# One decode block: cache and weight loads as long runs per partition, four heads per tile, one ring of buffers

## The chip, the cores and the metric

The kernel runs on one core of one Trainium2 chip. TensorE (PE) multiplies, VectorE (DVE) and ScalarE (ACT) do the elementwise work, GpSimd (POOL) builds a few constants, and SyncE (SP) issues the loads. All loads go from HBM to the on-chip memory (SBUF, 128 partitions) over 16 DMA engines. The metric is the device time of one execution in microseconds (us), as the median of several; lower is better.

## The reference

Two requests (B = 2) with one token each (D = 640) pass one transformer block whose norms are modulated by a condition `c`. Attention has 32 heads of 192 and looks at the last 1024 of 4096 cached positions.

```python
mod = (silu(c) @ w_mod).reshape(2, 6, 1, 640)      # sa, ca, ga, sb, cb, gb
h = layernorm(x) * (1 + ca) + sa
q = h @ wq                                          # 640 x 6144
k, v = k_cache[:, :, 3072:], v_cache[:, :, 3072:]   # 2 x 32 x 1024 x 192 each
p = softmax(einsum('bhqd,bhkd->bhqk', q, k) * 192 ** -0.5)
x = x + ga * (einsum('bhqk,bhkd->bhqd', p, v) @ wo) # wo 6144 x 640
h = layernorm(x) * (1 + cb) + sb
return x + gb * ((gelu(h @ w_gate) * (h @ w_up)) @ w_down)   # inner width 1536
```

All inputs are bf16. The part of the caches that is read is 50.3 MB; w_mod is 4.9 MB, wq and wo 7.9 MB each, and the three feed-forward weights 5.9 MB together.

## The kernel before

The kernel is written as lists of operations, one list per engine, in program order. A small tracker (`_Sched`, lines 27 to 101) adds the semaphore waits from what each operation reads and writes: buffers, ring slots and the eight banks of PSUM (the accumulation memory). Each engine runs its list strictly in order, SP too: a load that waits for a buffer holds every load behind it.

**Load order.** SP issues all loads through `k_dma` (line 242): c, x, the first third of w_mod (shift and scale of the first norm), wq in four column blocks, the rest of w_mod, then the caches through a ring, then wo in four row blocks, gate, up, and w_down in three pieces. wq and wo share one buffer (`r1`), w_mod and the feed-forward weights another (`r3`). A weight row with index k * 128 + p lies on partition p, so a partition gets one run of bytes per row and block.

**Ring.** `declare_ring` (line 260) fills 10 slots. One load brings one head of K or of V for both requests: partition p gets 8 consecutive positions (8 x 192 elements) of each request, two runs. K slots are released by the multiplies, V slots by the product with V.

**Start.** c and x are transposed on PE, the modulation is 150 matmuls with 128x128 weight tiles and 2 columns (line 328), then comes the norm. `q_unit` (line 347) computes q already repeated on all partitions: the normed x is copied into 128 columns (`hbc`, line 341), and five matmuls of 512 columns give 512 elements of q for one request (line 359); ACT copies them to `qbc`.

**A group** (16 of them) is two heads of both requests, four units. For each unit DVE multiplies K by q elementwise (line 396), and PE adds up over the 192 elements in three matmuls of 512 columns with an identity (line 408), which leave 64 sums per position; DVE adds these up for all four units at once (line 415). Then follow the maximum over the free axis (419), a transpose on PE (421), the maximum over the partitions (426), a diagonal matrix on ACT (428), its broadcast on PE (430), the subtraction (435) and the exponential (438). `p_pv` (line 441) multiplies with V, four units in four column strips of PE, and also sums the weights (454). One group later the result is divided (467, 469) and brought into rows by eight small matmuls (477, 478). `filler` (line 366) puts a unit of q, or later four matmuls whose result is not used, into gaps of PE. In the loop at line 488 the steps of three neighbouring groups are interleaved.

**End.** wo (line 546, 240 matmuls), the second norm, gate and up (line 564, 120), gelu, w_down (line 583, 60), a transpose of the result and its store.

Of the kernel before, what the change touches and what calls it, by code (L numbers as in the profile page):

```python
# [103 lines left out]
def bass_adaLN_cond__sliding_block_cached__geglu_ffn__decode_kernel(  # L104
# [13 lines left out]
    dbg=None,  # L118
):
    P = 128  # L120
# [5 lines left out]
    assert B == 2 and Dh == 192 and D % P == 0 and W % P == 0 and H % 2 == 0 and F % P == 0  # L126
    KT = D // P
    J = W // P
    NQ = H * Dh
    NT = NQ // P  # L130
    NG = H // 2
    FC = F // P
    SCALE = float(Dh) ** -0.5
    EPS = 1e-5
    GC = 512 // J
    NCH = Dh // GC
    assert J % 2 == 0 and GC * NCH == Dh and 2 * Dh + J <= 512
    ON = 2 * Dh

    NS = 10 if dbg is None else 8  # L140
    NP = 3
    HPC = 8 if H % 8 == 0 else 2
    NWQ = H // HPC
    CQ = HPC * Dh
    TPC = 12 if NT % 12 == 0 else 3
    NWO = NT // TPC
    WD_SPLIT = [FC // 2, FC - FC // 2 - max(1, FC // 6), max(1, FC // 6)] if FC >= 6 else [FC]
    WD_SPLIT = [n for n in WD_SPLIT if n > 0]
    QW = 512
    NQC = (NQ + QW - 1) // QW  # L150
    QUP = min(2 * NQC, 2 * ((3 * 2 * Dh + QW - 1) // QW))
    ND = 4

    es = ExitStack()
    with es:
        S = _Sched(nc, es)
        sb = lambda name, shape, dt: es.enter_context(nc.sbuf_tensor(name, shape, dt))

        r1 = sb("r1", [P, KT * NQ], BF16)
        wq_v = r1[:, :].rearrange("p (k n) -> p k n", k=KT)  # L160
        wo_v = r1[:, :].rearrange("p (t n) -> p t n", t=NT)
        R3N = max(KT * 6 * D + KT * 2 * P, 2 * KT * F + FC * D)
        r3 = sb("r3", [P, R3N], BF16)
        wm_v = r3[:, 0:KT * 6 * D].rearrange("p (k n) -> p k n", k=KT)
        hbc_v = r3[:, KT * 6 * D:KT * 6 * D + KT * 2 * P].rearrange("p (k b m) -> p k b m", k=KT, b=2)
# [3 lines left out]
        qbc = sb("qbc", [P, 2, NQ], BF16)  # L169
        ring = sb("ring", [P, NS, 2, J, Dh], BF16)  # L170
        prod = sb("prod", [P, NP, J, Dh], BF16)
# [4 lines left out]
        sel = sb("sel", [P, 8], BF16)  # L176
        xr = sb("xr", [2 * KT, P], BF16)
        cr = sb("cr", [2 * KT, P], BF16)
        scT = sb("scT", [P, KT, 2], BF16)
        X2 = sb("X2", [P, 2, KT, 2], F32)  # L180
# [3 lines left out]
        modT = sb("modT", [P, 6, KT, 2], F32)  # L184
        opc = sb("opc", [P, 2, KT, 2], F32)
        lnt = sb("lnt", [P, 2, KT, 2], F32)
        hT = sb("hT", [P, KT, 2], BF16)
        S_sb = sb("S_sb", [P, 2, 4, J], F32)
        Sb_sb = sb("Sb_sb", [P, 2, 4, J], F32)
        M1 = sb("M1", [P, 2, 4], F32)  # L190
        gmn = sb("gmn", [4, 2], F32)
        diag = sb("diag", [4, 2, 4], F32)
        E_sb = sb("E_sb", [P, 2, 4, J], BF16)
        den = sb("den", [P, 2], F32)
        junk = sb("junk", [P, 2, J], F32)
        rden = sb("rden", [P, 2], F32)
        On = sb("On", [P, 2, ON], BF16)
        oT = sb("oT", [P, NT, 2], BF16)
        h2T = sb("h2T", [P, KT, 2], BF16)
        gl = sb("gl", [P, FC, 2], F32)  # L200
        aT = sb("aT", [P, FC, 2], BF16)
        fin = sb("fin", [P, 2, KT, 2], F32)
        orow = sb("orow", [2 * KT, P], BF16)
        ps = es.enter_context(nc.psum_tensor("ps", [P, 8, 512], F32))

        BK_S = (0, 1, 2, 3)
        BK_T = 4
        FTC = 256
        BK_O = 5
        OTC = 2 * Dh + J + 8  # L210
        BK_Q = (6, 7)
# [7 lines left out]
        sem_wm = [S.sem("d_wm%d" % i) for i in range(2)]  # L219
        sem_wq = [S.sem("d_wq%d" % i) for i in range(NWQ)]  # L220
        sem_wo = [S.sem("d_wo%d" % i) for i in range(NWO)]
# [5 lines left out]
        dbg_sems = []  # L227
# [13 lines left out]
        def k_dma(dst, src):  # L241
            return lambda e: e.dma_start(dst, src)  # L242
# [7 lines left out]
        for i in range(NWQ):  # L250
# [4 lines left out]
                                    writes=["wm1"], name="ld_wm1"))  # L255

        ring_state = {"next": 0, "done": set()}
        NITEM = 4 * NG

        def declare_ring(consumed=()):  # L260
            ring_state["done"].update(consumed)
# [407 lines left out]
```

## Time and profile before

| | |
|---|---|
| median of 3 runs | 212.14 us (209.55 to 212.56) |
| profiled execution: span, first to last instruction | 207.9 us |
| profiled execution: its own time | the page gives none beside the span |
| read from HBM | 76.88 MB, 370 GB/s over the span |
| busy: PE, DVE, ACT | 134.0, 110.4, 43.5 us |
| mean granted clock of TensorE | 0.875 |

The profile is one execution recorded by the hardware. A group row gives line, engine, operation, output <- inputs, shape and count, then busy time and mean length of one, then idle time before it and what ended it. A row by stretches gives start:end, length, busy time and count for PE, PE weight loads, DVE, ACT and POOL, then the granted clock of TensorE, the DMA share, and GB/s. A row in order of time gives start, length, engine, line and operation, and how long the engine had been idle.

### The profile page before, as it was taken

The page shows a single profiled execution, that of the slowest core. Times are in us where ns is not written, and L with a number is a line of the kernel's source. Part 1 is how long each engine was busy: PE and PEld are TensorE (multiplying, and loading weights), DVE is VectorE, ACT ScalarE, POOL GpSimd, SP SyncE. Part 2 cuts the span into 40 slices and gives each one's busy share as a digit, 9 for nine tenths or more (in the row PEclk, how much of TensorE's full clock was granted, in tenths as well). Part 3 has the DMA queues.
Part 4 walks back from the last instruction along what each step waited for, and adds up shares of the span by engine and source line. Part 5 has one row for each costly group of instructions (what it writes and reads, how often), then busy time and mean ns, then how long its engine had stood idle before and what let it go on. Part 6 is the DMA issues. An engine that isn't in the chain of part 4 may idle for free.

```text
span 207.9 us, 3411 instructions
## 1 busy us (share of the span) xinstructions
PE 134.0 (64%) x1424; PEld 68.0 (33%) x1441; DVE 110.4 (53%) x176; ACT 43.5 (21%) x132; POOL 1.2 (1%) x9
## 2 busy tenths in 40 slices
PE   0229500696668869769687696696696694743443
PEld 0213200532333334324333243243243242643342
DVE  0050000439487876977869779779779765000300
ACT  2023300011423222232323221121121112400300
POOL 2000000000000000000000000000000000000000
PEclk9999955559999999999999999999999999555555
DMA  4999999999999999999999999999999999999990
GB/s 125 407 403 401 402 415 408 401 400 404 399 392 382 410 348 400 377 352 413 358 356 410 337 331 395 404 403 401 402 403 397 397 363 362 361 365 400 394 330 26
DMA packets 30523, 77.10 MB, mean 371 GB/s; under 512 B 1324, under 2 KB 9004, under 8 KB 30508
## 3 DMA queue, kind: packets, MB, share of 16 engines
q1 hardware_dynamic: 30508, 76.89, 97.7%
q8 instruction: 11, 0.18, 0.4%
q14 instruction: 4, 0.03, 0.0%
HBM read 76.88 MB, written 0.00 MB: 370 GB/s over the span
## 4 chain that ended last, share of the span: by engine, by line
PE 32%; SPq 32%; DVE 16%; DMA 13%; ACT 4%; issue 2%
SPq L242 32%; DVE S_sb L415 14%; PE ps L408 14%; DMA ring<-in_A_k_cache_dram 8%; DMA r<-in_B_w_down_dram 5%; PE ps L450 5%; PE ps L359 5%; PE ps L373 2%; ACT qbc L363 2%; PE ps L430 2%; PE ps L421 2%; PE ps L477 1%; DVE M L419 1%; ACT L438 1%; ACT E_sb L438 1%
## 5 line engine op out<-in xcount | busy, mean ns | idle before, releaser
L396 DVE TENSOR_TENSOR prod<-ring,qbc 128x1536 bf16<-128x1536 bf16 x64 | 59.3, 947 | 5.0 <-DMA ring<-in_A_k_cache_dram 5.0
L408 PE MATMUL ps<-prod,ident_b 128*128 128x512 bf16 x192 | 53.6, 391 | 1.8 <-DVE prod L396 1.8
L415 DVE TENSOR_REDUCE S_sb<-ps 128x32 f32<-128x2048 f32 x16 | 36.7, 2291 | 3.7 <-PE ps L408 3.7
L359 PE MATMUL ps<-r 128*128 128x512 bf16 x110 | 30.0, 413 | 4.3 <-DVE r L341 3.7
L363 ACT ACTIVATE qbc<-ps 128x512 bf16<-128x512 f32 x24 | 14.3, 597 | 43.8 <-PE ps L359 43.8
L408 PEld LDWEIGHTS ps<-prod,ident_b 128*128 128x128 bf16 x192 | 16.7, 99 | 18.4 <-issue 4.8
L421 PE MATMUL ps<-ident_f,M 128*4 128x128 f32 x16 | 4.3, 271 | 26.2 <-DVE M L419 26.2
L359 PEld LDWEIGHTS ps<-r 128*128 128x128 bf16 x120 | 11.9, 105 | 18.2 <-issue 4.6
L328 PE MATMUL ps<-scT,r 128*128 128x2 bf16 x150 | 4.3, 165 | 18.3 <-DMA r<-in_w_mod_dram 18.3
L450 PE MATMUL ps<-ring,E_sb 128*2 128x384 bf16 x256 | 13.7, 336 | 3.2 <-ACT E_sb L438 3.2
L381 DVE TENSOR_SCALAR opc<-modT 128x10 f32<-128x10 f32 x1 | 0.2, 173 | 24.7 <-ACT modT L333 24.7
L373 PE MATMUL ps<-qbc,ident_b 128*128 128x512 bf16 x49 | 12.9, 380 | 0.4
L421 PEld LDWEIGHTS ps<-ident_f,M 128*4 128x4 f32 x16 | 1.3, 81 | 34.1 <-DVE M L419 34.1
L467 DVE RECIPROCAL rden<-den 128x1 f32<-128x1 f32 x16 | 2.6, 164 | 18.4 <-ACT junk L462 18.4
L484 ACT ACTIVATE oT<-ps 128x6 bf16<-128x6 f32 x16 | 2.8, 176 | 37.9 <-PE ps L478 37.9
L328 PEld LDWEIGHTS ps<-scT,r 128*128 128x128 bf16 x150 | 4.2, 104 | 18.8 <-issue 18.8
L546 PE MATMUL ps<-oT,r 128*128 128x2 bf16 x240 | 6.9, 165 | 5.3 <-DMA r<-in_A_wo_dram 5.3
L469 ACT ACTIVATE On<-ps,rden 128x384 bf16<-128x384 f32 x16 | 9.2, 577 | 1.8 <-DVE rden L467 1.8
L450 PEld LDWEIGHTS ps<-ring,E_sb 128*2 128x2 bf16 x256 | 4.7, 82 | 12.5 <-ACT E_sb L438 7.2
L546 PEld LDWEIGHTS ps<-oT,r 128*128 128x128 bf16 x240 | 6.6, 104 | 5.4 <-DMA r<-in_A_wo_dram 5.4
L477 PE MATMUL ps<-sel,On 128*128 128x2 bf16 (+1 forms) x64 | 7.4, 183 | 1.2 <-ACT On L469 1.2
L462 ACT ACTIVATE junk<-ps 128x8 f32<-128x8 f32 x16 | 2.8, 177 | 23.0 <-PE ps L454 23.0
(64 smaller groups left out, 88.8 us busy)
## 6 DMA issues: line engine op xcount, KB each, us to landing
ring<-in_A_k_cache_dram SPq DMA_DIRECT2D x32, 768.0 KB, 6.5
ring<-in_A_v_cache_dram SPq DMA_DIRECT2D x32, 768.0 KB, 9.5
r<-in_A_wq_dram SPq DMA_DIRECT2D x4, 1920.0 KB, 17.8
r<-in_A_wo_dram SPq DMA_DIRECT2D x4, 1920.0 KB, 19.0
r<-in_w_mod_dram SPq DMA_DIRECT2D x1, 3200.0 KB, 24.4
r<-in_B_w_gate_dram SPq DMA_DIRECT2D x1, 1920.0 KB, 17.0
r<-in_B_w_up_dram SPq DMA_DIRECT2D x1, 1920.0 KB, 16.6
r<-in_w_mod_dram SPq DMA_DIRECT2D x1, 1600.0 KB, 6.9
```

What stands on the lines that cost most here:

```text
L242: return lambda e: e.dma_start(dst, src)
L359: last = e.matmul(ps[:, bk, 0:w], lhsT=hbc_v[:, k, b, :], rhs=wq_v[:, k, c0:c0 + w], start=(k == 0), stop=(k == KT - 1))
L363: S.op("act", lambda e: e.activation(out=qbc[:, b, c0:c0 + w], in_=ps[:, bk, 0:w], func=ACTF.Copy), reads=[bank(bk)], writes=[("qbc", cq, ...
L373: last = e.matmul(ps[:, BK_Q[0], 0:QW], lhsT=ident_b[:, :], rhs=qbc[:, 0, 0:QW], start=True, stop=True)
L396: return S.op("dve", lambda e: e.tensor_tensor(out=prod[:, pslot, :, :], in0=ring[:, ks, b, :, :], in1=qbc[:, b, h * Dh:(h + 1) * Dh].unsq ...
L408: last = e.matmul(o_ap, lhsT=ident_b[:, :], rhs=prod[:, pslot, :, ci * GC:(ci + 1) * GC], start=(ci == 0), stop=(ci == NCH - 1))
L415: S.op("dve", lambda e: e.tensor_reduce(out=S_sb[:, z, :, :], in_=ps[:, 0:4, 0:J * GC].rearrange("p k (j c) -> p k j c", j=J), axis=AX.X, ...
L421: S.op("pe", lambda e: e.transpose(ps[0:4, BK_T, 0:P], M1[:, z, :], ident_f[:, :]), reads=[("M1", z), "ident_f"], writes=[bank(BK_T)], nam ...
L450: e.matmul(ps[32 * i:32 * i + 2, BK_O, 0:ON], lhsT=E_sb[:, z, i, 2 * jp:2 * jp + 2], rhs=ring[:, vs, b, 2 * jp:2 * jp + 2, :], start=(jp = ...
L469: S.op("act", lambda e: e.activation(out=On[:, z, :], in_=ps[:, BK_O, 0:ON], func=ACTF.Identity, scale=rden[:, z:z + 1]), reads=[bank(BK_O ...
L477: e.matmul(o_ap, lhsT=On[:, z, c0:c0 + n], rhs=sel[:, s0:s0 + 2], start=True, stop=False, **kw)
L546: last = e.matmul(ps[:, BK_M, 2 * jn:2 * jn + 2], lhsT=wo_v[:, t, jn * P:(jn + 1) * P], rhs=oT[:, t, :], start=(t == 0 and jn == 0), stop= ...
```

## The change

**Loads.** A weight row with index p * KT + k (or p * FC + f, p * NT + t) now lies on partition p. So w_mod is one load with one run of 38400 bytes per partition, wq five loads of 12288 bytes (one row each), wo six of 10240 (eight rows), gate and up 15360, w_down 7680, 5120 and 2560. One load of K or V brings four heads of one request: partition 4 * p + h holds 32 consecutive positions of head h, 12288 bytes. c and x are loaded untransposed, issued by ACT instead of SP.

**One ring.** wq, K, V and wo share one ring of 8 slots of 12288 bytes per partition, in the order wq0 to wq4, K0, K1, V0, K2, V1, ..., K15, V14, V15, wo0 to wo5. Gate, up and w_down follow wo5 on SP, in the buffer of w_mod.

**Weights with a step.** As rows are spread differently, PE takes the columns of w_mod, wo and w_down with a step of 5 elements and those of gate and up with a step of 12.

**q.** The normed x (2 columns) is the stationary operand; 80 matmuls of 384 columns in four column strips put each head of a quad on its own strip, ACT and DVE copy them to rows, and 8 matmuls with a 0/1 matrix (`selq`) spread these over the partitions, one per group in the loop.

**A group** is four heads of one request; 16 groups again. The multiplies are three per group (16, 8 and 8 positions), the sums 3 x 12 matmuls of 256, 128 and 128 columns, one reduction over 512 elements instead of 2048. The four heads have one score per partition and position, and `mneg` (-1e30) removes the three foreign heads when the maximum is subtracted; ACT's exponential also adds up, and one matmul with a 0/1 matrix gives the denominator. P V is 16 matmuls. `p_sel` collects all groups in one bank (8 matmuls of 48 columns per group), copied once before wo. The filler matmuls are gone, and so is the transpose of the output, which is stored as 256 pieces of 10 bytes.

```diff
-    NS = 10 if dbg is None else 8
+    HQ = 4
+    PH = P // HQ
+    J = W // PH
+    NS = 8
+    SLOT = J * Dh
+    CHUNKS = [(0, J // 2), (J // 2, J // 4), (3 * J // 4, J // 4)]
...
+        items = [("wq", k) for k in range(KT)] + [("k", 0)]
+        for g in range(1, NG):
+            items += [("k", g), ("v", g - 1)]
+        items += [("v", NG - 1)] + [("wo", i) for i in range(NWO)]
+        slot_of = {it: n % NS for n, it in enumerate(items)}
...
+        def ring_src(it):
+            kind, i = it
+            if kind == "wq":
+                return A_wq.rearrange("(p k) n -> p k n", k=KT)[:, i, :], NQ
+            if kind == "wo":
+                return A_wo.rearrange("(p t) n -> p t n", t=NT)[:, i * WOT:(i + 1) * WOT, :].rearrange("p t n -> p (t n)"), WOT * D
+            quad, b = group(i)
+            src = A_k_cache if kind == "k" else A_v_cache
+            return src[b, quad * HQ:(quad + 1) * HQ, K0:Sk, :].rearrange("h (p j) d -> p h (j d)", p=PH), SLOT
...
+        S.dma("act", k_dma(rows[0:B, :], c[:, :]), sem_c, writes=["rows"], name="ld_c")
+        S.dma("act", k_dma(rows[B:2 * B, :], A_x.rearrange("b o d -> (b o) d")), sem_x, writes=["rows_x"], name="ld_x")
+        wm_dma = S.dma("sp", k_dma(wm_v.rearrange("p k n -> p (k n)"), w_mod.rearrange("(p k) n -> p (k n)", k=KT)), sem_wm,
+                       writes=["wm"], name="ld_wm")
+        declare_ring()
...
-                                            lhsT=wm_v[:, k, i * D + jn * P:i * D + (jn + 1) * P],
+                                            lhsT=wm_v[:, k, i * D:(i + 1) * D].rearrange("p (m j) -> p m j", j=KT)[:, :, j],
...
+        ln_mod("ln1", 0, 0, hT)
+        mod_part(1, 2, 6)
...
+                for n in range(NQB):
+                    for i in range(HQ):
+                        last = e.matmul(ps[32 * i:32 * i + B, n, 0:QW].rearrange("p (q d) -> p q d", d=Dh), lhsT=hT[:, k, :],
+                                        rhs=wv[:, 2 * n:2 * n + 2, i, :],
+                                        start=(k == 0), stop=(k == KT - 1), tile_position=(0, 32 * i))
...
+            S.op("pe", lambda e: e.matmul(ps[:, bk, 0:QW], lhsT=selq[:, b, :], rhs=qrow[:, n * QW:(n + 1) * QW], start=True, stop=True),
...
-                for ci in range(NCH):
-                    last = e.matmul(o_ap, lhsT=ident_b[:, :], rhs=prod[:, pslot, :, ci * GC:(ci + 1) * GC],
+                o_ap = ps[:, BK_S[z], j0 * GC:(j0 + nj) * GC].rearrange("p (j c) -> p j c", c=GC)
+                for t in range(NCH):
+                    last = e.matmul(o_ap, lhsT=ident_b[:, :], rhs=prod[:, z, j0:j0 + nj, t * GC:(t + 1) * GC],
...
+            S.op("dve", lambda e: e.tensor_tensor(out=Sb_sb[:, z, :, :], in0=S_sb[:, z, :].unsqueeze(2).broadcast_to([P, J, HQ]),
+                                                  in1=ps[:, BK_T, P:P + HQ].unsqueeze(1).broadcast_to([P, J, HQ]), op=ALU.add),
+                 reads=[("S", z), bank(BK_T)], writes=[("Sb", z)], name="sub_%d" % g)
+            S.op("act", lambda e: e.activation(out=E_sb[:, z, :, :], in_=Sb_sb[:, z, :, :], func=ACTF.Exp, scale=SCALE,
+                                               accum_out=denp[:, z:z + 1]),
...
+                for jp in range(NPAIR):
+                    i = jp % 4
+                    last = e.matmul(ps[32 * i:32 * i + 2 * HQ, BK_O, 0:ON],
+                                    lhsT=E_sb[:, z, 2 * jp:2 * jp + 2, :].rearrange("p j h -> p (j h)"),
+                                    rhs=ring[:, sl, 2 * jp * Dh:(2 * jp + 2) * Dh],
+                                    start=(jp < 4), stop=(jp >= NPAIR - 4), tile_position=(0, 32 * i))
...
             if has:
                 d_mul(g, 0)
+                p_reduce(g, 0)
             if pp:
-                chain_b2(g - 2)
+                c_rec(g - 2)
+            if prev:
+                c_sum(g - 1)
             if has:
                 d_mul(g, 1)
                 p_reduce(g, 1)
             if prev:
-                chain_a2(g - 1)
+                c_max2(g - 1)
+                c_bc(g - 1)
             if has:
                 d_mul(g, 2)
+                declare_ring([("k", g)])
                 p_reduce(g, 2)
+            if prev:
+                c_exp(g - 1)
+                p_den(g - 1)
+            q_unit()
+            if pp:
+                p_sel(g - 2)
+            if prev:
                 p_pv(g - 1)
+                declare_ring([("v", g - 1)])
...
+                wv = ring[:, slot_of[("wo", ci)], 0:WOT * D].rearrange("p (t m j) -> p t m j", t=WOT, j=KT)
+                        last = e.matmul(ps[:, BK_M, 2 * j:2 * j + 2], lhsT=wv[:, tl, :, j], rhs=oT[:, t, :],
...
+        S.dma("sp", k_dma(wg_v.rearrange("p k n -> p (k n)"), B_w_gate.rearrange("(p k) n -> p (k n)", k=KT)), sem_wg,
+              writes=["wg"], deps=r3_dead, name="ld_wg")
...
+                                        lhsT=wv[:, k, :].rearrange("p (m f) -> p m f", f=FC)[:, :, fc],
...
+        S.dma("sp", k_dma(out.rearrange("b o (p j) -> p (b o) j", j=KT), finb[:, :, :]), sem_out, reads=["finb"], name="st_out")
```

More of the change, by code (lines that the diff above doesn't have):

```diff
@@ L445, in f, with p_sel @@
+        def p_sel(g):
+            z = g % 2
+            quad, b = group(g)
             def f(e):
                 last = None
[L447 to L452 removed]
```

563 lines of the change are left out of this document (249 added, 314 removed).

## The prediction

> **What bounds the kernel now.** I read the page's slices and DMA queue first: is the core short of data or of compute?
>
> ```profile
> span 207.9 us, 3411 instructions
> DMA  4999999999999999999999999999999999999990
> DMA packets 30523, 77.10 MB, mean 371 GB/s; under 512 B 1324, under 2 KB 9004, under 8 KB 30508
> q1 hardware_dynamic: 30508, 76.89, 97.7%
> HBM read 76.88 MB, written 0.00 MB: 370 GB/s over the span
> ```
>
> The load queue is busy for 97.7% of the span and no packet of it reaches 8 KB. So the time is 76.88 MB divided by a rate, and the question is where the rate is lost. The table by stretches answers that; its last three columns are TensorE's granted clock, DMA share and GB/s.
>
> ```profile
> 12.00:17.00 5.00, 2.08 (x5) 0.89 (x7) 2.02 (x8) 0.33 (x2) 0.00 (x0) 1.00 1.03 402
> 30.00:33.00 3.00, 0.00 (x0) 0.00 (x0) 0.00 (x0) 0.00 (x0) 0.00 (x0) 0.50 1.02 416
> 60.00:90.00 30.00, 24.64 (x199) 11.14 (x204) 23.20 (x33) 8.28 (x28) 0.00 (x0) 1.00 1.00 386
> 90.00:120.00 30.00, 23.22 (x186) 10.41 (x181) 23.43 (x33) 8.54 (x29) 0.00 (x0) 1.00 0.98 367
> 120.00:155.00 35.00, 27.82 (x232) 12.47 (x234) 28.45 (x40) 6.29 (x27) 0.00 (x0) 1.00 1.02 392
> 170.00:172.00 2.00, 1.95 (x26) 0.89 (x26) 0.35 (x2) 0.67 (x3) 0.00 (x0) 1.00 1.07 363
> 3.50:4.00 0.50, 0.00 (x0) 0.00 (x0) 0.00 (x0) 0.00 (x0) 0.00 (x0) 1.00 0.62 174
> 201.00:202.00 1.00, 0.30 (x12) 0.21 (x9) 0.18 (x1) 0.00 (x0) 0.00 (x0) 0.50 0.95 316
> 203.00:204.00 1.00, 0.40 (x15) 0.32 (x13) 0.00 (x0) 0.00 (x0) 0.00 (x0) 0.50 0.23 86
> ```
>
> The stretches differ in the length of the contiguous run that one descriptor moves. By the code wq moves runs of 3072 bytes (12 to 17 us: 402 GB/s), the second part of w_mod 5120 (30 to 33: 416), wo 1280 (170 to 172: 363). One engine of 16 thus needs 16 x 1280 / 363 = 56.4 ns for a 1280-byte run and 16 x 3072 / 402 = 122.3 ns for 3072: 36.8 ps per byte and a fixed 9.3 ns per run. For 5120 bytes this gives 197.6 ns, or 415 GB/s, against the row's 416. Two parameters fit three rows.
>
> Per engine the kernel moves 76.88 MB / 16 = 4.805 MB, hence 176.7 us of bytes, in 1824 runs (K and V 1024, wo 384, wq 160, w_down 96, w_mod 80, gate and up 80): 17.0 us. Together 193.7. The stretches from 60 to 155 lie under 402 by 16, 35 and 10 GB/s: 30 x 16/402 + 30 x 35/402 + 35 x 10/402 = 4.7 us lost. Their sum, 198.4, matches the stretch at full rate, from about 3.5 to about 202. The 4.7 us have this cause:
>
> ```profile
> SPq L93 <- PE ps L454: 80.0, 13, 8.9
> ```
>
> The loading queue waits 13 times, 80 us in total, for the P V product to give back its two V slots, and not always soon enough. After 202 the engines run dry one by one; the end of the chain of waits, in start, length and what, is
>
> ```profile
> 193.83 10.79 DMA r<-in_B_w_down_dram
> 204.67 0.44 PE ps L583 x10
> 205.57 0.39 PE ps L595
> 205.98 0.27 ACT orow L597
> ```
>
> So 5.9 us pass between the end of the full rate and 207.9. The page gives no time of the profiled execution beside its span; the median of the runs, 212.14, is 4.2 above the span, and I add these 4.2.
>
> **The change, part by part: the loads.** K, V and wq now come in runs of 12288 bytes, wo 10240, w_mod 38400, gate and up 15360, w_down 7680, 5120 and 2560. Per engine that is 8 runs per load: 8 x (32 K and V + 5 wq + 6 wo + w_mod + gate + up + 3 w_down) = 392, and 3.6 us in place of 17.0. The bytes stay. Stream: 176.7 + 3.6 = 180.3 us. A run over 5120 bytes is not in the trace: above, the fit may not hold and 416 is the best there is (76.88 MB / 416 = 184.8 us); below, the fixed part vanishes (176.7). I take 180.3, as three rows lie on the line. The bytes of c and x move to the ACT queue, so SP's first large load goes out earlier:
>
> ```profile
> 0.81 0.40 SPq L242 DMA_DIRECT2D cr<-in_c_dram  x1
> 1.59 0.40 SPq L242 DMA_DIRECT2D r<-in_w_mod_dram  x1
> ```
>
> That is 0.8 us; the two ACT issues delay only Silu, which the matmuls need when w_mod is in, 11 us later. The stream starts at about 2.8.
>
> [...]
>
> **The waits in one ring.** Eight slots of 1.57 MB, each 8 x (12288 x 36.8 ps + 9.3 ns) = 3.69 us. After w_mod (14.2 us) wq lands by 32.6, K0 at 36.3, K1 at 40.0, V0 at 43.7, then a pair every 7.38. The new wait: SP holds K2 until wq0's slot is read, and every later load queues behind it. It must be issued by about 41. PE reads wq after both modulation products and the norm's two last steps; the products took 1.47 + 2.81 us before,
>
> ```profile
> 8.58 1.47 PE L328 MATMUL ps<-scT,r 128*128 128x2 bf16 x50 [5.76 <-DMA r<-in_w_mod_dram]
> 36.07 2.81 PE L328 MATMUL ps<-scT,r 128*128 128x2 bf16 x100 [12.50 <-DMA r<-in_w_mod_dram]
> ```
>
> so wq0 is read at about 21, 20 us in time, and wq4 by 34. Later, K(g+4) needs K(g)'s slot about 25 us after K(g) lands. gate, up and w_down queue behind wo5, whose slot is K15's, read at about 148 while the queue still holds loads until 165. So no wait of the ring is late if a group's compute is under 7.38 us:
>
> ```profile
> L396 DVE TENSOR_TENSOR prod<-ring,qbc 128x1536 bf16<-128x1536 bf16 x64 | 59.3, 947 | 5.0 <-DMA ring<-in_A_k_cache_dram 5.0
> L415 DVE TENSOR_REDUCE S_sb<-ps 128x32 f32<-128x2048 f32 x16 | 36.7, 2291 | 3.7 <-PE ps L408 3.7
> L419 DVE TENSOR_REDUCE M<-S_sb 128x4 f32<-128x32 f32 x16 | 3.0, 186 | 0.5
> L426 DVE TENSOR_REDUCE gmn<-ps 4x1 f32<-4x128 f32 x16 | 4.3, 271 | 0.4 <-PE ps L421 0.4
> L435 DVE TENSOR_TENSOR Sb_sb<-S_sb,ps 128x32 f32<-128x32 f32 x16 | 3.0, 188 | 6.6 <-PE ps L430 6.6
> L467 DVE RECIPROCAL rden<-den 128x1 f32<-128x1 f32 x16 | 2.6, 164 | 18.4 <-ACT junk L462 18.4
> 40.69 2.74 PE L408 MATMUL ps<-prod,ident_b 128*128 128x512 bf16 x6 [1.82 <-DVE prod L396]
> 50.47 1.58 PE L408 MATMUL ps<-prod,ident_b 128*128 128x512 bf16 x6
> 55.77 0.82 PE L450 MATMUL ps<-ring,E_sb 128*2 128x384 bf16 x16 [1.58 <-ACT E_sb L438]
> 176.33 1.41 PE L450 MATMUL ps<-ring,E_sb 128*2 128x384 bf16 x16 [0.54 <-ACT E_sb L438]
> ```
>
> DVE: the three multiplies cover what four did, at most 4 x 0.947 = 3.79; the sum over 512 in place of 2048 elements is 2.29 / 4 plus a fixed part up to 0.19, 0.76; then 0.19, 0.27, about 0.3 for a subtraction four times as wide, 0.16. In all 5.5 us, 1.4 less than before. PE: 36 identity matmuls over the same 6144 columns, 2 x 1.58 = 3.2 at full clock; P V 0.82; q, selection and the single-column steps about 1.5, an estimate from the 0.2 to 0.4 us of such pieces. In all 5.5. They wait on each other twice per group (maximum, then broadcast), so I take 6 to 6.5 us per group: hidden, by 0.9 or more. q falls from 120 wide matmuls to 80 narrow and 8 spreading ones and the filler matmuls go; nothing on the path becomes shorter by it. Gain: the 4.7 us.
>
> **The end.** wo5 lands at 169.3, gate 173.9, up 178.4, w_down 183.1. The output loses the transpose and its copy (0.39 + 0.27) but stores 256 pieces of 10 bytes for 10 of 256; between 0.7 gained and 1.3 lost, I take nothing.
>
> New in the last products and in the modulation are weights read with a step of 5 or 12 elements. The nearest rows are a dense bf16 load in sequence, and a pair of dense fp32 loads:
>
> ```profile
> 189.75 1.76 PE L546 MATMUL ps<-oT,r 128*128 128x2 bf16 x60 [3.60 <-DMA r<-in_A_wo_dram]
> L546 PEld LDWEIGHTS ps<-oT,r 128*128 128x128 bf16 x240 | 6.6, 104 | 5.4 <-DMA r<-in_A_wo_dram 5.4
> 192.18 0.50 PEld L289 LDWEIGHTS ps<-X,ones_f 128*128 128x128 f32 x2 [0.75 <-DVE X L287]
> 195.23 1.76 PE L564 MATMUL ps<-h2T,r 128*128 128x2 bf16 x60 [2.43 <-DVE h2T L317]
> ```
>
> Dense, a load and matmul take 1.76 / 60 = 29 ns each; one load alone lasts 104, an fp32 one 250. I take 29 to 60. Forty per wo chunk then need at most 2.4 us and the chunk's landing 3.1: hidden.
>
> **Sum.** 2.8 + 180.3 + 5.9 = 189.0 us of span, plus 4.2: **193 us**, against 212.14. By differences: 13.4 (runs) + 4.7 (ring) + 0.8 (start) = 18.9 less.
>
> **Rivals.** (1) Strided weights become the bound. If one costs x, PE starts wo at about 153.8 and needs 420 x in the end (240 wo, 120 gate and up, 60 down), the norm between (191.5 to 195.2 before: 3.7), 0.9 for the activations and 3.2 at the end: time 165.8 + 420 x. It overtakes the loads at 65 ns, is level with before's median at 110, and 2% slower from 120; at 250 it gives 271. For it: no row shows such a load, and 104 is a real duration. Against it: dense loads run one per 29 ns at half clock, 3.6 times less than one lasts. Chance 0.13, half of it above 100 ns.
>
> [...]
>
> (2) TensorE at half clock. The fillers held it busy 24.64 of 30 us; now it is about 5.5 of 7.4. The rows at 0.50 cost 2 x 2.74 + 1.41 + about 2.3 = 9.2 us per group: 36.3 + 16 x 9.2 + 4 + 420 x 0.029 + 3.7 + 0.9 + 3.2 = 207.5, time 212. Against it: at 9.2 PE would hardly pause, and such work brought the clock back before:
>
> ```profile
> 40.00:47.00 7.00, 6.09 (x15) 2.30 (x17) 3.31 (x5) 0.60 (x1) 0.00 (x0) 0.52 1.03 400
> 47.00:60.00 13.00, 8.05 (x53) 3.12 (x52) 9.94 (x13) 4.34 (x9) 0.00 (x0) 1.00 1.03 396
> ```
>
> 6.09 us busy of 7 at 0.52, and from 47 on 1.00 with 8.05 of 13. Chance 0.07.
>
> (3) K and V loads over four heads are slower: one load now touches four places 1.57 MB apart. They are 50.3 MB, 118 us of the stream; they make the kernel 2% slower (216.4) once they take 141, at 357 GB/s. Nothing in the trace speaks for it but that it is untested. Chance 0.06.
>
> (4) The long runs bring nothing beyond the best row: 416 GB/s throughout, 198 us. Chance 0.16.
>
> **Numbers.** Forecast 0.58. A measurement of this kernel tells about 2% from no change. Below 207.9: forecast, (4), nearly half of (1) and a little of the rest, 0.81. Within 2%: (2) and a slice of (1), 0.08. Slower: the top of (1) and (3), 0.11. The range runs from 188 (no fixed cost per run: 3.6 less, and 1 at the end) to 207, which takes in (4) and (1) below 98 ns; about 0.2 lies outside.
>
> **What would show it.** Right: 425 GB/s or more from 5 to about 182 us, 7.4 us between K loads, no SP wait that lets the DMA share fall, the last landing some 5 us before the end. Wrong: K and V stretches under 410; PE busy without pause behind landed weights after 155 (rival 1, read off the spacing of the wo matmuls); a clock of 0.5 with groups of 9 us (rival 2).

## The result and the profile after

The changed kernel takes 194.89 us (194.76 to 194.98 in four runs), the kernel before beside it 211.95 (209.55 to 212.56, now four runs). The ratio is 0.921, with a 95% interval of 0.915 to 0.926: 8% faster. The forecast was 193.0. The profiled execution took 194.89 us, with a span of 193.1.

The page of the changed kernel, its slices of DMA share, its packets and its load queue:

```profile
span 193.1 us, 3891 instructions
DMA  7999999999999999999999999999999999999910
DMA packets 7353, 77.13 MB, mean 399 GB/s; under 512 B 1060, under 2 KB 1064, under 8 KB 1448
q1 hardware_dynamic: 7328, 76.88, 94.7%
```

The same 76.88 MB now come in 7328 packets instead of 30508, and the queue is still the busy resource. The table by stretches (columns as before, the last three are clock, DMA share and GB/s) shows the rate:

```profile
17.00:36.00 19.00, 11.35 (x185) 6.24 (x183) 0.83 (x5) 0.53 (x3) 0.00 (x0) 1.00 1.01 428
60.00:90.00 30.00, 22.89 (x279) 17.25 (x278) 20.05 (x35) 5.40 (x15) 0.00 (x0) 0.92 1.01 424
120.00:150.00 30.00, 21.54 (x254) 16.04 (x252) 18.71 (x32) 3.93 (x12) 0.00 (x0) 0.89 1.01 424
182.00:184.00 2.00, 2.00 (x37) 2.00 (x35) 0.00 (x0) 0.00 (x0) 0.00 (x0) 0.50 0.73 297
184.00:185.00 1.00, 1.00 (x20) 1.00 (x19) 0.00 (x0) 0.00 (x0) 0.00 (x0) 0.50 0.41 155
```

In the caches' stretches it is 424 GB/s, where the kernel before had 386, 367 and 392. Full rate ends at about 182 us instead of about 202. The waits (engine, line, what for: total us, times, longest) still have SP on top:

```profile
SPq L93 <- DVE prod L419: 70.2, 16, 5.8
SPq L93 <- PE ps L484: 28.1, 14, 2.4
SPq L93 <- PE ps L382: 27.5, 5, 17.1
SPq L619 <- DMA out_dram<-finb: 3.4, 1, 3.4
```

SP waits 98 us for the slots of the caches and 27.5 for those of wq, more than the 80 of before, and yet the DMA share stays at 1.01: by the page a cache load is issued 25 us before it lands (median), so loads are still under way while SP waits. Here the length of a wait says little; the DMA share beside it does. In order of time, K multiplies and the end:

```profile
86.17 1.76 DVE L419 TENSOR_TENSOR prod<-ring,qbc 128x3072 bf16<-128x3072 bf16 x1 [1.22 <-DMA ring<-in_A_k_cache_dram]
93.56 1.76 DVE L419 TENSOR_TENSOR prod<-ring,qbc 128x3072 bf16<-128x3072 bf16 x1 [2.16 <-DMA ring<-in_A_k_cache_dram]
...
172.50 1.76 PE L556 MATMUL ps<-oT,ring 128*128 128x2 bf16 x40 [1.33 <-DMA ring<-in_A_wo_dram]
...
177.77 3.75 PE L587 MATMUL ps<-h2T,r 128*128 128x2 bf16 x60 [2.23 <-DVE h2T L338]
...
181.80 3.75 PE L587 MATMUL ps<-h2T,r 128*128 128x2 bf16 x60 [0.27 <-DMA r<-in_B_w_up_dram]
...
185.89 2.56 PE L606 MATMUL ps<-aT,r 128*128 128x2 bf16 x60 [0.35 <-DVE aT L598]
...
188.90 0.40 SPq L231 DMA_DIRECT2D out_dram<-finb  x1
```

A pair of loads takes 7.39 us and DVE waits for K each time. The end looks different from before: gate, up and down are nearly one unbroken run of TensorE from 177.77 to 188.45, with 0.3 us at a landing and at one elementwise product between them. The gate product still ends just before up lands; up and down are late. The last load, w_down's third piece, is issued at 153.8 us and lands 32.6 later, at 186.4, but the store goes out only at 188.90 (before: 204.62 and 206.27). After the store is issued another 4.2 us pass until 193.1 (before: 206.27 to 207.9, 1.6). The w_down loads of the changed kernel (durations, first and last start; then KB and us to landing), and the store before:

```profile
L231 SPq DMA_DIRECT2D r<-in_B_w_down_dram x3: 432/432/827, 152.5 to 153.8; - x3
r<-in_B_w_down_dram SPq DMA_DIRECT2D x1, 320.0 KB, 32.6
```

```profile
206.27 0.33 SPq L242 DMA_DIRECT2D out_dram<-orow  x1
```

One reason stands in the weight-load groups (busy, mean ns of one); before, those of the same products had 104 or 105 ns:

```profile
L556 PEld LDWEIGHTS ps<-oT,ring 128*128 128x128 bf16 x240 | 10.0, 131 | 5.8 <-DMA ring<-in_A_wo_dram 5.2 <-issue 0.6
L587 PEld LDWEIGHTS ps<-h2T,r 128*128 128x128 bf16 x120 | 7.3, 164 | 2.7 <-DVE h2T L338 2.3 <-DMA r<-in_B_w_up_dram 0.4
```

Per load with its matmul, step 5 takes 1.76 / 40 = 44 ns (2.56 / 60 = 43 in the last product), step 12 takes 3.75 / 60 = 63, dense 1.76 / 60 = 29 as before.

### The profile page after: what moved, and what is told of

Its sections match the earlier page's. It is cut to its first block, busy times and chain, and to the rows that moved or that the text cites. A ratio compares the mean times of both kernels' runs of the same rounds, so it can differ in the third digit from the quotient of the medians.

```text
span 193.1 us, 3891 instructions
## 1 busy us (share of the span) xinstructions
PE 124.5 (64%) x1723; PEld 95.2 (49%) x1723; DVE 86.4 (45%) x164; ACT 28.3 (15%) x70; POOL 2.6 (1%) x12
## 3 DMA queue, kind: packets, MB, share of 16 engines
q1 hardware_dynamic: 7328, 76.88, 94.7%
HBM read 76.88 MB, written 0.00 MB: 398 GB/s over the span
## 4 chain that ended last, share of the span: by engine, by line
DMA 81%; DVE 6%; PE 6%; issue 3%; SPq 1%; DVEq 0%
DMA ring<-in_A_k_cache_dram 53%; DMA r<-in_B_w_up_dram 15%; DMA ring<-in_A_wq_dram 13%; DVE prod L419 4%; PE ps L587 2%; PE ps L432 1%; PE ps L606 1%; SPq L231 1%; DVE S_sb L439 1%; PE ps L382 1%; DVE nmx L449 0%; DVE M L442 0%; DVE rden L493 0%; DVE aT L598 0%; DVE finb L615 0%
## 5 line engine op out<-in xcount | busy, mean ns | idle before, releaser
L432 PE MATMUL ps<-prod,ident_b 128*128 128x128 bf16 (+1 forms) x576 | 59.1, 261 | 28.1 <-DVE prod L419 28.0
L419 DVE TENSOR_TENSOR prod<-ring,qbc 128x1536 bf16<-128x1536 bf16 (+1 forms) x48 | 58.1, 1214 | 26.4 <-DMA ring<-in_A_k_cache_dram 26.4
L432 PEld LDWEIGHTS ps<-prod,ident_b 128*128 128x128 bf16 x576 | 45.3, 108 | 42.4 <-DVE prod L419 37.8
L556 PE MATMUL ps<-oT,ring 128*128 128x2 bf16 x240 | 10.4, 179 | 5.3 <-DMA ring<-in_A_wo_dram 4.9
L484 PE MATMUL ps<-ring,E_sb 128*8 128x384 bf16 x256 | 13.4, 330 | 0.0
L556 PEld LDWEIGHTS ps<-oT,ring 128*128 128x128 bf16 x240 | 10.0, 131 | 5.8 <-DMA ring<-in_A_wo_dram 5.2
L382 PE MATMUL ps<-ring,hT 128*2 128x384 bf16 x80 | 7.1, 517 | 7.2 <-DMA ring<-in_A_wq_dram 7.2
L439 DVE TENSOR_REDUCE S_sb<-ps 128x32 f32<-128x512 f32 x16 | 10.8, 673 | 1.3 <-PE ps L432 1.3
L587 PE MATMUL ps<-h2T,r 128*128 128x2 bf16 x120 | 7.5, 199 | 2.5 <-DVE h2T L338 2.2
L587 PEld LDWEIGHTS ps<-h2T,r 128*128 128x128 bf16 x120 | 7.3, 164 | 2.7 <-DVE h2T L338 2.3
```

Source lines behind the costliest of these rows:

```text
L382: last = e.matmul(ps[32 * i:32 * i + B, n, 0:QW].rearrange("p (q d) -> p q d", d=Dh), lhsT=hT[:, k, :], rhs=wv[:, 2 * n:2 * n + 2, i, :], ...
L419: S.op("dve", lambda e: e.tensor_tensor(out=prod[:, z, j0:j0 + nj, :], in0=ring[:, sl, j0 * Dh:(j0 + nj) * Dh].rearrange("p (j d) -> p j d ...
L432: last = e.matmul(o_ap, lhsT=ident_b[:, :], rhs=prod[:, z, j0:j0 + nj, t * GC:(t + 1) * GC], start=(ci == 0 and t == 0), stop=(t == NCH - ...
L439: S.op("dve", lambda e: e.tensor_reduce(out=S_sb[:, z, :], in_=ps[:, BK_S[z], :].rearrange("p (j c) -> p j c", c=GC), axis=AX.X, op=ALU.ad ...
L484: last = e.matmul(ps[32 * i:32 * i + 2 * HQ, BK_O, 0:ON], lhsT=E_sb[:, z, 2 * jp:2 * jp + 2, :].rearrange("p j h -> p (j h)"), rhs=ring[:, ...
L556: last = e.matmul(ps[:, BK_M, 2 * j:2 * j + 2], lhsT=wv[:, tl, :, j], rhs=oT[:, t, :], start=(t == 0 and j == 0), stop=(t == NT - 1), skip ...
```

## The experiments

The theory is that of the prediction: the time is the bytes plus a fixed cost per run, the ring never starves the queue, and what is left is the end. The rivals: ring and shorter groups brought the gain; loads over four heads behave differently; and, for the end, that only the last landing counts. The kernels ran in three groups of four, each on one chip: the two run lengths, dense gate and up, and the store as rows; four slots, one and three multiplies, and everything dense; step 4, step 4 with dense weights, five multiplies, and the changed kernel once more. It took 193.92 us there, against 194.89 in the first measurement; so kernels are compared within a group, or by their ratio to the kernel before. In the two profiled executions this difference lies behind the issue of the store: it goes out at 188.94 and 188.90, but SP then waits 2.5 us for it instead of 3.4. So where two kernels store in the same way, the issue of the store compares them better than the time. The second measurement:

```profile
188.94 0.41 SPq L231 DMA_DIRECT2D out_dram<-finb  x1
SPq L619 <- DMA out_dram<-finb: 2.5, 1, 2.5
```

### Run lengths of before, all else changed

```diff
+        NCUT = 4
+        RUN_WQ, RUN_WM, RUN_WO, RUN_GU, RUN_WD = 3072, 2560, 1280, 3072, 1280
...
+            return lambda e: e.dma_start(dst, src, max_dma_last_dim=run)
...
+            w = SLOT // NCUT
...
+                for i in range(NCUT):
+                    d = e.dma_start(dst[:, i * w:(i + 1) * w], src[:, :, i * w:(i + 1) * w])
```

> The changed kernel, with every load cut again to the run lengths of the kernel before: K, V and wq 3072 bytes (K and V as four loads per tile), w_mod 2560, wo 1280, gate and up 3072, w_down 1280. Order, ring, q, groups and end stay. Runs per DMA engine go from 392 to 1864. Theory of the prediction (9.3 ns per run): 1472 x 9.3 ns = 13.7 us more, so 194.9 + 13.7 = 208.6, with the K and V stretches at 402 GB/s. Rival A (the gain came from the ring and the shorter groups, and run length does not matter): 195 to 196, the K and V stretches still at 424. Rival B (a load over four heads is slower at the same run length): the K and V stretches under 395 GB/s and over 212 us.

Measured: 207.01 us, 0.978 of before (0.974 to 0.982). The load queue's packets on the page:

```profile
q1 hardware_dynamic: 32416, 76.89, 98.2%
```

By stretches:

```profile
60.00:90.00 30.00, 20.53 (x250) 15.66 (x251) 19.44 (x32) 5.41 (x15) 0.00 (x0) 0.94 1.03 400
```

In order of time, the product with up:

```profile
195.19 3.76 PE L609 MATMUL ps<-h2T,r 128*128 128x2 bf16 x60 [1.11 <-DMA r<-in_B_w_up_dram]
```

Per engine (32416 - 7328) / 16 = 1568 packets were added: the 1472 runs and one for each of 96 additional loads. The cache stretch falls to 400 (402 was the fit), so four heads in one load cost at most half a percent of their own: rival (3) of the prediction is out. Up's weights are in 13.4 us later than in the changed kernel (195.19 against 181.80), with 1496 of the added packets ahead of them (72 are w_down's): 9.0 ns each, where the fit had 9.3. The time itself rises by 12.1 us against the first measurement of the changed kernel and by 13.1 against the second, whose store took as long as here (2.5 us); 13.7 were expected. So most of the gain goes away with this one property. What stays is that of the ring and the earlier start. The kernel before, in order of time:

```profile
199.54 1.76 PE L564 MATMUL ps<-h2T,r 128*128 128x2 bf16 x60 [2.56 <-DMA r<-in_B_w_up_dram]
```

It started up 4.35 us later, and it has (32416 - 30508) / 16 = 119 packets per engine less than this one, 1.1 us: 5.4 us together, 5.5 predicted. Both numbers come from the profiled execution of before, which was a quick one; where its slower executions lose their time is not known.

### Half the dose

```diff
+        NCUT = 2
+        RUN_WQ, RUN_WM, RUN_WO, RUN_GU, RUN_WD = 6144, 5120, 5120, 5120, 2560
```

> The changed kernel with a middle dose: K, V and wq in runs of 6144 bytes (K and V as two loads per tile), w_mod, wo, gate and up 5120, w_down 2560. Runs per engine 844 instead of 392, so 452 more. Theory (a fixed 9.3 ns per run): + 4.2 us, 199.1, that is 0.31 of what the kernel with the old run lengths loses; K and V at 414 GB/s. Rival (a threshold between 3072 and 12288 bytes, or a loss that stands only on the shortest runs): within 1 us of 194.9, or as long as the kernel with the old run lengths.

Measured: 197.91 us, 0.935 of before (0.931 to 0.939). The load queue on the page, then a row by stretches and one in order of time:

```profile
q1 hardware_dynamic: 15136, 76.88, 96.1%
```

```profile
60.00:90.00 30.00, 22.55 (x268) 16.75 (x267) 19.24 (x33) 5.14 (x16) 0.00 (x0) 0.90 1.02 416
```

```profile
185.91 3.78 PE L609 MATMUL ps<-h2T,r 128*128 128x2 bf16 x60 [0.49 <-DMA r<-in_B_w_up_dram]
```

The rate is 416 (414 expected), and up starts 4.1 us later: 4.1 / 13.4 = 0.31 of the full dose, the share that was expected. The time itself rises by 3.0 and 4.0 us against the two measurements of the changed kernel; 4.2 were expected. (15136 - 7328) / 16 = 488 packets per engine were added, 24 of them w_down's: 4.1 / 464 = 8.8 ns each. The three lengths show no threshold between 3072 and 12288 bytes: each run costs the same, 8.8 to 9.0 ns.

### Four slots instead of eight

```diff
-    NS = 8
+    NS = 4
```

> The changed kernel with 4 ring slots instead of 8. Theory (the stream never waits, because a group is done within the 7.4 us of a pair of loads; four slots still leave SP's issue about 5 us ahead of the end of the queue): 194.9 to 197, the K and V stretches at 420 or more. Rival (the depth of the ring is what took away the 4.7 us of waits): SP's waits now let the DMA share fall, by about 1 us or more per group, 203 to 215.

Measured: 194.02 us, 0.924 of before (0.919 to 0.929), so no loss. By stretches:

```profile
90.00:120.00 30.00, 22.75 (x278) 17.03 (x276) 20.25 (x34) 3.93 (x12) 0.00 (x0) 0.91 1.01 423
```

The rate holds with half the slots, so their number is not what keeps the queue full. That a group is done well within the time of its loads is left as the reason, and the next test bears on it. Which part of the new ring took the waits of before away, its order, its common slots for K and V or the shorter group, was not tested one by one.

### How much room a group has

```diff
             if has:
                 d_mul(g, 1)
+                for _r in range(1):
+                    S.op("dve", lambda e, g=g, sl=slot_of[("k", g)]: e.tensor_tensor(
+                        out=spare[:, :, :], in0=ring[:, sl, 0:J // 4 * Dh].rearrange("p (j d) -> p j d", d=Dh),
...
```

With range(1), range(3) and range(5):

> The changed kernel with one more multiply of 1536 elements per group on DVE (0.95 us, result unused), between the second multiply and the maximum. Theory (DVE waits 1.65 us per group for K; the DMA queue is the bound): 194.9, within 0.4. Rival (the group's compute is already the bound): 16 x 0.95 = 15.2 us more, 210.

> The changed kernel with three more such multiplies per group (2.84 us). Theory: 1.65 us of it fit into the wait for K, and some of the 0.3 us in which DVE waits for the transposed maximum; the remaining 0.9 to 1.2 us come 16 times: 209 to 214, DVE no longer waiting for K, SP's waits letting the DMA share fall. Rival (the ring's eight slots and the waits hide more than that): under 200.

> The changed kernel with five more multiplies of 1536 elements per group on DVE. With three a group took 7.53 us in the trace, 0.16 over the 7.37 us between two K loads, and the time rose by about 1.5 us. Theory (DVE is the bound from there on): 2 x 0.95 us more for each of 16 groups, 30.4 us over the kernel with three: 225 to 227, with the DMA share falling to about 0.8 in the groups. Rival (there is more room that the trace doesn't show): under 215.

Measured: 193.86, 195.43 and 228.34 us; against before 0.923 (0.919 to 0.927), 0.930 (0.926 to 0.935) and 1.082 (1.073 to 1.091). One multiply costs nothing, as expected. Three cost about 1.5 us and not 15 to 19: this expectation was wrong, and its rival held. Five went a little beyond the 225 to 227 expected. With three, in order of time:

```profile
82.44 1.74 DVE L420 TENSOR_TENSOR prod<-ring,qbc 128x3072 bf16<-128x3072 bf16 x1
...
89.97 1.74 DVE L420 TENSOR_TENSOR prod<-ring,qbc 128x3072 bf16<-128x3072 bf16 x1
```

DVE no longer waits between these two multiplies: a group lasts 7.53 us. Of it the three multiplies are 2.94, so the group's own work is 4.6 us, and the room 7.4 - 4.6 = 2.8 us, not the 1.65 us of idle time that the page puts down to K. Most of the rest was idle time that the page puts down to PE:

```profile
L449 DVE TENSOR_REDUCE nmx<-ps 1x4 f32<-1x128 f32 x16 | 4.5, 278 | 4.7 <-PE ps L444 4.7
```

In this row of the changed kernel DVE waits 4.7 us in all for the transposed maxima, and 6.4 more before the subtraction; a multiply ahead of them fills that time too. The loads do not feel it yet. By stretches, with three:

```profile
90.00:120.00 30.00, 22.07 (x264) 16.33 (x263) 29.54 (x44) 3.93 (x12) 0.00 (x0) 0.89 1.01 424
```

DVE only falls behind them, by about 0.15 us per group and 2.4 over 16 groups; part of this is made up in the wait for wo's landings, and the store goes out 1.6 us later than in the changed kernel (190.48 against 188.90). With five, by stretches:

```profile
90.00:120.00 30.00, 21.83 (x206) 15.87 (x203) 29.28 (x41) 3.44 (x10) 0.00 (x0) 0.72 0.93 344
```

Now DVE is busy 29.28 of 30 us, the rate falls to 344 GB/s, and two more multiplies add 32.9 us (from one group of runs to another, between which the kernel before itself differs by about one percent), that is 2.06 per group of heads for 1.9 of work. So compute decides from about 7.4 us per group on, and in the changed kernel DVE's work is 2.8 us away from it.

### Dense weights for gate and up

```diff
-        wd_src = B_w_down.rearrange("(p f) n -> p f n", f=FC)
+        wd_src = B_w_down.rearrange("(f p) n -> p f n", f=FC)
...
-                                        lhsT=wv[:, k, :].rearrange("p (m f) -> p m f", f=FC)[:, :, fc],
+                                        lhsT=wv[:, k, fc * P:(fc + 1) * P],
```

> The changed kernel, with the weights of gate and up read dense (128 neighbouring columns per weight load) instead of with a step of 12; for that the rows of w_down lie on the partitions as before the change (row f * 128 + p), in runs of 1280 bytes, 72 runs more per engine. Theory: the two products stand on the path at the end, since up ends 3.8 us after its weights have landed, and a weight load with its matmul goes from 63 to 29 ns: up then ends 2 us sooner (120 x 34 ns = 4.1 us are saved, but up waits for its landing), less 0.7 us for the runs: 192.5 to 194. Rival (the step costs nothing on the path, the end is set by the last landing and the store): 195.0 to 195.6.

Measured: 194.46 us, 0.919 of before (0.916 to 0.922), hardly less than the 0.921 of the changed kernel. This lies between the theory (192.5 to 194) and the rival (195.0 to 195.6); SP waited 3.6 us for the store in this execution. In order of time:

```profile
182.04 1.76 PE L586 MATMUL ps<-h2T,r 128*128 128x2 bf16 x60 [2.27 <-DMA r<-in_B_w_up_dram]
...
184.71 1.33 PE L605 MATMUL ps<-aT,r 128*128 128x2 bf16 x30 [0.91 <-DMA r<-in_B_w_down_dram]
186.23 1.36 PE L605 MATMUL ps<-aT,r 128*128 128x2 bf16 x30 [0.18 <-DMA r<-in_B_w_down_dram]
...
188.04 0.39 SPq L231 DMA_DIRECT2D out_dram<-finb  x1
```

Gate and up go back to 29 ns and up ends 1.7 us sooner, as the theory has it. But now the last product waits for w_down, whose shorter runs also come later, and the store goes out only 0.9 us sooner. The step did stand on the path, but with these runs the last landing takes over after 0.9 us: the theory had left it out.

### Step 4 instead of 12, with long runs

```diff
-    WD_SPLIT = [(0, 6), (6, 4), (10, 2)]
+    FS = 4
+    WD_SPLIT = [(0, 4), (4, 4), (8, 2), (10, 2)]
...
-        wd_src = B_w_down.rearrange("(p f) n -> p f n", f=FC)
+        wd_src = B_w_down.rearrange("(o p f) n -> o p f n", p=P, f=FS)
...
-                                        lhsT=wv[:, k, :].rearrange("p (m f) -> p m f", f=FC)[:, :, fc],
+                                        lhsT=wv[:, k, :].rearrange("p (o m f) -> p o m f", m=P, f=FS)[:, fc // FS, :, fc % FS],
```

> The changed kernel, with the inner width of the feed-forward part spread so that the weights of gate and up are read with a step of 4 elements instead of 12: column 512 o + 4 m + f of gate and up, and row 512 o + 4 p + f of w_down, with w_down in runs of 5120, 5120, 2560 and 2560 bytes (8 runs more per engine, 0.1 us). So far, per load and matmul: dense 29 ns, step 5 43 ns, step 12 63 ns. If the price grows with the step, step 4 takes 38 to 41 ns; if two elements in 16 bytes are enough for full speed, 29 ns. In time: up then ends 1.3 to 1.8 us sooner, the w_down product follows at once, so 1.3 to 1.8 us less than the changed kernel on the same chip. Rival (the last landing of w_down takes over at once, as with the dense weights): 0.4 us less.

> The changed kernel itself, as the reference for the others on the same chip: 194 to 195.

Measured on the same chip: 192.71 us (192.55 to 192.86) against 193.92 (193.7 to 194.2) for the changed kernel: 1.2 us less, just under the 1.3 to 1.8 expected. Against before: 0.912 (0.907 to 0.918) and 0.918 (0.913 to 0.924). In order of time, and the weight loads' group:

```profile
178.18 2.17 PE L588 MATMUL ps<-h2T,r 128*128 128x2 bf16 x60 [2.23 <-DVE h2T L339]
...
184.61 2.74 PE L607 MATMUL ps<-aT,r 128*128 128x2 bf16 x60 [0.35 <-DVE aT L599]
```

```profile
L588 PEld LDWEIGHTS ps<-h2T,r 128*128 128x128 bf16 x120 | 4.2, 118 | 4.2 <-DVE h2T L339 2.3 <-DMA r<-in_B_w_up_dram 1.8
```

Step 4 takes 2.17 / 60 = 36 ns: less than the 38 to 41 that the other steps suggested, more than dense. So a load lasts 104, 118, 131 and 164 ns at steps 1, 4, 5 and 12, and one per 29, 36, 43 and 63 ns is reached. The other value of the expectation, full speed at step 4, was a guess and did not hold: it is 7 ns short of the dense 29. The price grows with the step over all four.

### The store as rows

```diff
-        S.dma("sp", k_dma(out.rearrange("b o (p j) -> p (b o) j", j=KT), finb[:, :, :]), sem_out, reads=["finb"], name="st_out")
+        S.op("pe", lambda e: e.transpose(ps[0:B * KT, BK_T, 256:256 + P], finb[:, :, :].rearrange("p b j -> p (b j)"), ident_f[:, :]),
...
+        S.op("act", lambda e: e.activation(out=orow[:, :], in_=ps[0:B * KT, BK_T, 256:256 + P], func=ACTF.Copy),
...
+        S.dma("sp", k_dma(out.rearrange("b o (j p) -> (b o j) p", p=P), orow[:, :]), sem_out, reads=["orow"], name="st_out")
```

> The changed kernel with the end of the kernel before: the result is transposed on TensorE, copied by ACT and stored as ten rows of 256 bytes instead of 256 pieces of 10 bytes. The elements of the output then stand at permuted places; nothing else changes. Theory: the store, now 3.8 us from issue to landing, goes back to 1 to 1.6 us, and transpose and copy cost 0.7: net 1.5 to 2.3 us less, 192.6 to 193.4. Rival (the prediction's value, store net zero): 194.9; what lies behind 188.9 us is then not the store's pieces.

Measured: 193.11 us, 0.913 of before (0.910 to 0.916). In order of time, and SP's wait for the store:

```profile
188.73 0.18 DVE L616 TENSOR_TENSOR finb<-fin,X 128x10 f32<-128x10 f32 x1
...
189.67 0.37 SPq L232 DMA_DIRECT2D out_dram<-orow  x1
```

```profile
SPq L624 <- DMA out_dram<-orow: 0.9, 1, 0.9
```

The store is issued 0.8 us later (189.67 against 188.90), but SP waits 0.9 us for it instead of 3.4, and the span is 191.3 instead of 193.1: 1.8 less. This was a long wait: in the other profiled executions with the 256 pieces it was 2.2 to 3.6 us, so the net price of the pieces lies between 0.5 and 1.9 us; by the ratios alone, 0.913 against 0.921 and 0.918, the intervals touch. Why the wait varies was not found.

### Everything dense, and the best of both

The first kernel joins the dense gate and up and the store as rows with dense weights elsewhere; x, the rows of wq and those of gate and up are spread to match:

```diff
-                                            lhsT=wm_v[:, k, i * D:(i + 1) * D].rearrange("p (m j) -> p m j", j=KT)[:, :, j],
+                                            lhsT=wm_v[:, k, i * D + j * P:i * D + (j + 1) * P],
...
-        S.dma("sp", k_dma(wg_v.rearrange("p k n -> p (k n)"), B_w_gate.rearrange("(p k) n -> p (k n)", k=KT)), sem_wg,
+        S.dma("sp", k_dma(wg_v, B_w_gate.rearrange("(k p) n -> p k n", p=P)), sem_wg,
...
-                        last = e.matmul(ps[:, BK_M, 2 * j:2 * j + 2], lhsT=wv[:, tl, :, j], rhs=oT[:, t, :],
+                        last = e.matmul(ps[:, BK_M, 2 * j:2 * j + 2], lhsT=wv[:, tl, j * P:(j + 1) * P], rhs=oT[:, t, :],
```

The second has all of this but takes gate, up and w_down from the kernel with step 4 (gate and up in runs of 3072 bytes).

> The changed kernel with the long runs kept where they cost TensorE nothing: K, V, wq, wo and w_mod as they are, but all weight loads of TensorE dense (modulation, wo, gate, up, w_down), gate and up in runs of 3072 bytes, w_down 1280, and the output transposed and stored as ten rows of 256 bytes. 136 runs more per engine: + 1.3 us of stream. Theory (up and down stand on the path, and so does the store): up ends 0.3 us behind its landing plus 1.8, down 1.8 after that at most, the store 2 us shorter: 190.5 to 192. Rival (only the stream counts): 194.9 + 1.3 = 196.2.

> The kernel with dense weights and the output stored as rows, but gate and up with a step of 4 and w_down in runs of 5120 and 2560 bytes again instead of 1280. 64 runs per engine (0.6 us) fall away against it, all of them behind wo, where the last landing was the bound; up takes 0.5 us longer but then ends before w_down lands. Theory: 0.4 to 0.6 us less than that kernel, that is 1.8 to 2.6 us less than the changed kernel on the same chip. Rival (the end hangs on wo's last landing alone): as the kernel with dense weights, 1.2 us less than the changed kernel.

Measured: 192.66 us for the first, 0.917 of before (0.914 to 0.920); 192.34 (192.16 to 192.45) for the second, 0.911 (0.904 to 0.917). On its chip the second is 1.6 us faster than the changed kernel, the fastest of all that were run there. Both gained less than expected (190.5 to 192 for the first, 1.8 to 2.6 us less than the changed kernel for the second). The second, in order of time:

```profile
182.64 2.16 PE L590 MATMUL ps<-h2T,r 128*128 128x2 bf16 x60 [2.67 <-DMA r<-in_B_w_up_dram]
...
187.27 0.43 PE L609 MATMUL ps<-aT,r 128*128 128x2 bf16 x10 [0.33 <-DMA r<-in_B_w_down_dram]
...
188.87 0.38 SPq L234 DMA_DIRECT2D out_dram<-orow  x1
```

The rows of gate and up in 3072-byte runs bring up 0.5 us later than with step 4 alone (182.64 against about 182.1), and the last piece of w_down, awaited until 187.27, lands 0.8 us later than in the changed kernel. TensorE is then no longer late: it waits for this landing, and the store goes out 1.6 us behind it, as before the change. What was gained on TensorE and at the store is partly paid back in runs. The first kernel waits in the same way, until 187.54.

## Why the prediction was right, and where it was wrong

**Runs: right.** 13.4 us were taken for 1432 runs fewer, at 9.3 ns. The two run-length experiments give 9.0 and 8.8 ns, and (30508 - 7328) / 16 = 1449 packets fewer at 9.0 make 13.0 us. The line through three rows held outside them: 12288 bytes were to give 16 x 12288 / (452.2 + 9.3) = 426 GB/s, and the rows have 424 to 428. The sign named for it, 425 or more, was missed by 1 in the caches' stretches. So rival (4), nothing beyond 416, is out.

**Ring: right.** 4.7 + 0.8 us were taken for ring and start, 5.4 were found, both in one quick execution of before. That the old ring and groups lost the 4.7 is shown by the 400 GB/s at the old run lengths, where before had 386, 367 and 392; that they lost it by SP's waits alone is not, as the DMA share of before falls less there (0.98 against 1.03) than the rate. No wait of SP lowers the DMA share now (1.01 in the groups), as argued. The reason given, that a group's work fits into 7.38 us, agrees with the added multiplies: at 7.53 us per group the loads still come at 424 GB/s, at 9.6 they fall to 344. DVE's part of a group was taken at 5.5 us and is 4.6; the whole group, with the waits of the engines on each other, was taken at 6 to 6.5 and takes 7.39 - 1.65 = 5.7 (without the wait for K).

**End of full rate: right.** 2.8 + 180.3 = 183.1 was predicted, about 182 is seen. The last landing, which lay 2.6 us behind it before (202 to 204.62), would so be due at 185.7; it came at 186.4. The landings that the prediction gives one by one (wo5 169.3, up 178.4, w_down 183.1) are running sums of the stream; in the trace they come 3.2 to 3.4 us later (172.5, 181.8, 186.4), though the rate is as forecast.

**The end: wrong.** The term of 5.9 us, carried over from the kernel before, failed: from 182 to 193.1 it is 11.1 us. Counted from the last landing it is clearer: from there to the end 3.3 us were due (204.62 to 207.9), and 6.7 passed (186.4 to 193.1). Of these 3.4 us more, about 1.6 are TensorE and 1.8 the store.

TensorE: the store is issued 2.5 us behind the last landing. Before it was 1.65, of which some 0.8 were the transpose and the copy that are now gone. The delay comes from the strided weights. Their price was an estimate and nearly held (29 to 60 ns taken, 43 and 63 measured), but "hidden" was worked out only for wo, whose landings are 3.1 us apart. Gate's 60 loads are covered too, by up's landing; up's 60 at 63 ns start only when up has landed, w_down's 60 at 43 ns follow, and no landing behind them is late enough to cover that: 3.75 + 2.56 us, where dense ones take 1.76 each. Step 4 in place of 12 gave 1.1 us of the store's issue back (187.80 against 188.94), and with w_down dense as well the store was again bound to the last landing. Rival (1) had asked whether TensorE falls behind from 153.8 on; with the measured prices its formula gives 165.8 + 240 x 0.044 + 120 x 0.063 + 60 x 0.043 = 186.5, and it does not. The case between, covered for wo and gate and bare after them, was not among the rivals.

The store: it took 2.6 us more behind its issue (4.2 against 1.6), of which the dropped transpose and copy give 0.8 back. The prediction put the change at "between 0.7 gained and 1.3 lost, I take nothing"; the 1.3 was an estimate that no row of before shows. Over all profiled executions it is 0.5 to 1.9 lost, 1.8 in this one.

**Around the span: wrong the other way.** 4.2 us were added to the span because the median of before lay that far over its profiled span. Here 194.89 - 193.1 = 1.8. In every execution whose span is on record, of all kernels, the time lies 1.7 to 1.9 us over the span. So 207.9 + 1.8 = 209.7 belongs to the fastest of the runs of before (209.55 to 212.56): the profile showed a quick execution, and the difference to the median was scatter between executions, not time around the span. This error of 2.4 us hid more than half of the 4.1 us by which the span was forecast too short (193.1 against 189.0). That the total is only 1.9 us off is in part luck.

**The clock: as hoped, not tested.** Rival (2) feared half clock in the groups. It was 0.92 and 0.89 in the two stretches shown between 60 and 150. With five multiplies on DVE, when TensorE had fewer matmuls to do in the same time (206 in 30 us, against 279 and 254), it fell to 0.72; what would happen at 0.5 throughout was not tried.

## What to carry to other kernels

Where loads are the bound, fit the rate of stretches with different run lengths to bytes plus a fixed cost per run; here two rows gave both numbers (36.8 ps per byte and 9.3 ns per run), a third agreed, and they forecast longer runs well (426 GB/s against 424 to 428). Then cost the last products separately from the stream: here the layout that suits the loads made the weights and the output strided, and that was free where a later landing covered it (wo, gate) and cost 3.4 us behind the last one, about 1.6 on TensorE and 1.8 at the store. To find the room of an engine, add work to it until the time moves; idle time put down to one cause was only part of it here (1.65 us of 2.8).

## What was not expected of the hardware

Two small loads came late beside a long one. c and x, 2.5 KB each, go through ACT's queue, issued in the changed kernel at 0.80 and 1.37 us, and the first transpose waits for x until 7.26:

```profile
0.80 0.54 ACTq L231 DMA_DIRECT2D rows<-in_c_dram  x1
...
7.26 0.33 PE L300 MATMUL ps<-ident_b,rows 4*128 4x4 bf16 x5 [7.26 <-DMA rows<-in_A_x_dram]
```

That the 38400-byte runs of w_mod, issued at the same time on SP's queue, hold them up is likely but was not tested by itself. It fits that x was in sooner where w_mod came in shorter runs, at 5.95 us with 5120 bytes and at 5.62 with 2560; there the other loads were cut too. It costs nothing here, since w_mod itself is awaited until 15.05.

A weight load with a step of 5 has the same price at both clocks. In order of time, the first modulation product, at a granted clock of 1.00 (5 to 17 us):

```profile
15.05 2.13 PE L359 MATMUL ps<-scT,r 128*128 128x2 bf16 x50 [6.17 <-DMA r<-in_w_mod_dram]
```

That is 2.13 / 50 = 43 ns at step 5, and 2.56 / 60 = 43 in the last product, at 0.50.
